# Routed attention and a quick-gelu feed-forward on one core: scores with the keys on the partitions, and two heads side by side

## The chip, the cores and the metric

The kernel runs on one core of a Trainium2 chip. The metric is the device time in microseconds of one launch.

## What is computed

The reference is an attention in which a query sees only the keys of its own cluster, and behind it a feed-forward block without routing:

```python
# q, k, v: (4, 8, 768, 64); centroids: (8, 16, 64); all normal numbers times 0.1
q_assign = argmax(normalised(q) @ normalised(centroids).T)     # also k_assign
mask = q_assign[:, :, :, None] == k_assign[:, :, None, :]
scores = np.where(mask, q @ k.T / 8, -1e9)
attn = exp(scores - max(scores)); attn /= sum(attn) + 1e-9
x = (attn @ v).transpose(0, 2, 1, 3).reshape(3072, 512)
h = x @ w_in                                                   # 512 x 2048
out = (h * sigmoid(1.702 * h)) @ w_out                         # 2048 x 512
```

Everything is float32, except that the two weight matrices come as float64 words.

## The kernel before, in words

There are 4 batches of 8 heads. Two heads are a pair; 16 pairs, 4 to a batch. A sequence is 6 tiles of 128 tokens, two halves of 384. A unit is one query tile of one head, so a pair has 12 units (UP) and the whole kernel 192 (NU).

Engines: TensorE (PE) multiplies and transposes, VectorE (DVE) and ScalarE (ACT) read its results out of PSUM, GpSimd (POOL) works on SBUF alone, SyncE (SP) issues the loads and stores. Each takes its instructions in the order in which the program below emits them (`manual_schedule`); only waits for data and for free buffers shift them.

Preparation of a pair (`PREP`, eleven steps, one per turn of the loop): `prep_qk` (L199) turns q and k so that the head dimension lies on the partitions, `prep_assign` (L218) multiplies each token tile with the 16 centroids of its head (24 matmuls of 16 columns) and finds the largest on DVE, `prep_hot` (L241) turns the one-hot codes and puts them as 16 extra rows under q and k. A matmul over 80 rows then gives the score, lowered by 2^100 where the clusters differ.

A unit: `scores` (L277) makes 128 queries x 768 keys in two matmuls of 384 columns. `softmax` takes the row maximum on DVE (L286), scales it (L288), and ACT writes the exponential and its row sum (L292). `normalise` divides: a reciprocal on DVE (L303), a scaling of all 768 columns on POOL (L304). `turn` (L314) transposes the six 128 x 128 blocks on PE, and ACT (L319) and DVE (L321) copy them out. `values` (L333) multiplies six value tiles, 64 columns wide, with the six blocks; ACT copies the result into x transposed (L336).

Feed-forward (FFN): when a batch is complete, 56 chunks are queued: 32 of `first` (L351: four matmuls of 384 columns, tanh on ACT L356, product on DVE L359) and 24 of `second` (L370: four matmuls of 512 columns; every fourth is followed by a copy L376 and a store). They use two PSUM banks of their own.

Weights come in 64 chunks of 128 x 256. `round_w` makes float32 of each in nine steps that go to and fro between the engines: DVE L130, L132, POOL L135, DVE L141, POOL L137, L139, DVE L143, L145, POOL L147. One or two chunks are done in each turn until all 64 are (in the 43rd turn), so that all of it lies in batch 0, where no FFN work exists yet.

The loop fixes the order of everything. In turn u it emits the scores of unit u, the scaling of u - 1, the transposes of u - 2, the softmax of u, then as many FFN chunks as are owed (4/3 a turn), the values of u - 3, one preparation step for the next pair, and the weights:

```python
    for u in range(NU + 3):
        ...
            scores(u)
        ...
            normalise(u - 1)
        ...
            turn(u - 2)
        ...
            softmax(u)
        owed = owed + rate if ffn else 0.0
        while owed >= 1.0 and ffn:
            ffn.popleft()()
            owed -= 1.0
        if u >= 3:
            values(u - 3)
        if p + 1 < NPAIR and r < len(PREP):
            PREP[r](p + 1)
```

So units 0 to 47 run without FFN work, the others with that of the batch before, and the FFN of the last batch is left for the end.

Of the kernel before, what the change touches and what calls it, by code (L numbers as in the profile page):

```python
# [8 lines left out]
FP32 = mybir.dt.float32  # L9
BF16 = mybir.dt.bfloat16  # L10
I32 = mybir.dt.int32
U32 = mybir.dt.uint32
# [2 lines left out]
AX = mybir.AxisListType  # L15


@with_exitstack
def kernel(
    ctx: ExitStack,  # L20
    tc: tile.TileContext,
    q: bass.AP,
# [4 lines left out]
    moe_w_out: bass.AP,  # L27
    out: bass.AP,
):
    """Routed attention, then x -> quick-gelu(x @ w_in) @ w_out, all in float32.  # L30

    The weights come as the 64-bit words of float64 numbers, which no engine
    computes with, and are rounded to float32 on the chip.

    Token s of a (batch, head) sits on partition s // NJ, at place s % NJ, so
    that each partition loads one contiguous run. Token tiles are the NJ places.
    """
    nc = tc.nc

    B, H, S, D = q.shape  # L40
    NC = centroids.shape[1]
    DM, DF = moe_w_in.shape
    P = 128
    NJ = S // P            # token tiles of a sequence
    HALF = S // 2          # score columns in one PSUM bank
    NH = NJ // 2           # token tiles of a half
    HP = H // 2            # head pairs
    NPAIR = B * HP
    NCH = DM // P
    NF = DF // P  # L50
    KA = D + NC            # contraction rows of the scores
    SLOT = 32              # columns of a one-hot code in its transpose
    SCALE = D ** -0.5
    # A key of another cluster gets -FAR added to its raw score, and the sum
    # rounds to -FAR exactly: its softmax weight is 0 next to any key of the
    # query's cluster, and where there is none all weights are equal.
    FAR = float(2 ** 100)
    assert D == 64 and NC == 16 and H * NC == P and NJ == 6 and DM == H * D

# [13 lines left out]
    ps_f = ctx.enter_context(tc.tile_pool(name="ps_f", bufs=2, space=PS))  # L73
    ctx.enter_context(tc.manual_schedule())

# [1 line left out]
    qk_in, v_in = {}, {}  # L77

    def pair_src(src, p):
# [4 lines left out]
    def load_qk(p):  # L84
        for w, src in enumerate((q, k)):
            t = inp.tile([P, 2, NJ, D], FP32, name=f"in{w}")
            nc.sync.dma_start(out=t.rearrange("p a j d -> p a (j d)"),
                              in_=pair_src(src, p))
            qk_in[p, w] = t

    def load_v(p):
        t = inp.tile([P, 2, NJ, D], FP32, name="inv", bufs=3)
        nc.sync.dma_start(out=t.rearrange("p a j d -> p a (j d)"),
                          in_=pair_src(v, p))
        v_in[p] = t
# [7 lines left out]

    w_in = const.tile([P, NCH, DF], FP32, name="w_in")
    w_out = const.tile([P, NF, DM], FP32, name="w_out")
    WN = 256               # weights per partition in a chunk
    w_chunks = [
        (w[:, c, n:n + WN],
         src.bitcast(I32)[c * P:(c + 1) * P, 2 * n:2 * (n + WN)])
# [10 lines left out]
            w_raw[i] = t  # L120

    def round_w(i):
        """float64 words to float32: +-2^k (a power in float32, 0 or inf past
        its range) times 1.m, of m the 20 high bits exactly, the rest rounded."""
        raw = w_raw.pop(i)
        hi, lo = raw[:, :, 1], raw.bitcast(U32)[:, :, 0]
        m, e, one_m = (hp_pool.tile([P, HALF], FP32, name="g")[:, 0:WN]
                       for _ in range(3))
        m, e = m.bitcast(I32), e.bitcast(I32)
        nc.vector.tensor_scalar(out=m, in0=hi, scalar1=0xFFFFF, scalar2=None,  # L130
                                op0=ALU.bitwise_and)
        nc.vector.tensor_scalar(out=e, in0=hi, scalar1=20, scalar2=0x7FF,  # L132
                                op0=ALU.logical_shift_right,
                                op1=ALU.bitwise_and)
        nc.gpsimd.tensor_scalar(out=one_m, in0=m, scalar1=2.0 ** -20,  # L135
                                scalar2=1.0, op0=ALU.mult, op1=ALU.add)
        nc.gpsimd.tensor_scalar(out=e, in0=e, scalar1=896 + 255.0,  # L137
                                scalar2=896.0, op0=ALU.min, op1=ALU.max)
        nc.gpsimd.tensor_scalar(out=e, in0=e, scalar1=-896.0, scalar2=1.0,  # L139
                                op0=ALU.add, op1=ALU.mult)  # L140
        nc.vector.scalar_tensor_tensor(out=one_m, in0=lo, scalar=2.0 ** -52,  # L141
                                       in1=one_m, op0=ALU.mult, op1=ALU.add)
        nc.vector.tensor_scalar(out=e, in0=e, scalar1=23, scalar2=None,  # L143
                                op0=ALU.logical_shift_left)
        nc.vector.scalar_tensor_tensor(out=e, in0=hi, scalar=-2 ** 31, in1=e,  # L145
                                       op0=ALU.bitwise_and, op1=ALU.bitwise_or)
        nc.gpsimd.tensor_tensor(out=w_chunks[i][0], in0=one_m,  # L147
                                in1=e.bitcast(FP32), op=ALU.mult)

    for i in range(3):  # L150
        load_w(i)

# [1 line left out]
    ident = const.tile([P, P], FP32, name="ident")  # L154
    masks.make_identity(nc, ident)
    ident_h = const.tile([P, P], BF16, name="ident_h")
    nc.vector.tensor_copy(out=ident_h, in_=ident)
    half = const.tile([P, 1], FP32, name="half")
    nc.vector.memset(half, 0.5)
    # NC - c for cluster c: the largest among equals is the first of them.  # L160
    rank = const.tile([P, NC], FP32, name="rank")
    nc.gpsimd.iota(rank, pattern=[[-1, NC]], base=NC, channel_multiplier=0,
                   allow_small_or_imprecise_dtypes=True)
    # One-hot codes before their transpose; the columns past NC stay 0.
    hot = [const.tile([P, NJ * 4, SLOT], BF16, name=f"hot{i}")
           for i in range(2)]
    for t in hot:
        nc.vector.memset(t, 0.0)

    # Normalised centroids, transposed: [D, H * NC].  # L170
    csq = const.tile([P, D], FP32, name="csq")
    css = const.tile([P, 1], FP32, name="css")
    nc.vector.tensor_tensor(out=csq, in0=cent, in1=cent, op=ALU.mult)
# [11 lines left out]
    nc.tensor.transpose(out=cps[0:D, 0:P], in_=csq, identity=ident)  # L185
    nc.vector.tensor_copy(out=cT, in_=cps[0:D, 0:P])

    # ---- operands of the scores: rows 0:D are q^T or k^T, rows D:KA the
    # cluster one-hot of a query, or FAR below 0 off the cluster of a key ----
    aug = {}  # L190

    def prep_qk(p, i):
# [13 lines left out]
            nc.vector.tensor_copy(out=dst, in_=ps[0:D, 0:HALF])  # L206

    def prep_assign(p):
        """The cluster of each token, as a one-hot code. The norm of q or k
        scales a token's NC products alike, so their order needs none."""  # L210
        hp = p % HP
        ps = ps_t.tile([P, 512], FP32, name="t")
        sc = ps[:, 0:NJ * 4 * NC].rearrange("p (n c) -> p n c", c=NC)
        for j in range(NJ):
            for w in range(2):
                for a in range(2):
                    c0 = (2 * hp + a) * NC
                    nc.tensor.matmul(  # L218
                        out=sc[:, 4 * j + 2 * w + a, :],
                        lhsT=aug[p, a][0:D, w, j * P:(j + 1) * P],  # L220
                        rhs=cT[:, c0:c0 + NC], start=True, stop=True)
        n = NJ * 4
        best = asg.tile([P, n], FP32, name="best")
        nc.vector.tensor_reduce(out=best, in_=sc, axis=AX.X, op=ALU.max)
        eq = asg.tile([P, n, NC], FP32, name="eq")
        nc.vector.tensor_tensor(
            out=eq, in0=sc, in1=best[:, :, None].broadcast_to((P, n, NC)),
            op=ALU.is_equal)
        nc.vector.tensor_tensor(
            out=eq, in0=eq, in1=rank[:, None, :].broadcast_to((P, n, NC)),  # L230
            op=ALU.mult)
        first = asg.tile([P, n], FP32, name="first")
        nc.vector.tensor_reduce(out=first, in_=eq, axis=AX.X, op=ALU.max)
        nc.vector.tensor_tensor(
            out=hot[p % 2][:, :, 0:NC], in0=eq,
            in1=first[:, :, None].broadcast_to((P, n, NC)), op=ALU.is_equal)
# [21 lines left out]
    PREP = [lambda p, i=i: prep_qk(p, i) for i in range(8)]  # L258
    PREP += [prep_assign, lambda p: None, prep_hot]

# [1 line left out]
    UH = NJ  # L262
    UP = 2 * NJ
    NU = NPAIR * UP
# [57 lines left out]
        AT_of[u] = AT  # L322

    def values(u):
        """A query tile's part of x^T: rows are model dims, columns tokens."""
        p, a, qt = split(u)
        AT = AT_of.pop(u)
        if a == 0 and qt == 0:
            xT_of[p] = xp.tile([P, S], FP32, name="xT", bufs=2 * NCH)
        O = ps_t.tile([P, 512], FP32, name="t")  # L330
        rows = slice(a * D, (a + 1) * D)
        for kt in range(NJ):
            nc.tensor.matmul(out=O[rows, 0:P], lhsT=v_in[p][:, a, kt, :],  # L333
                             rhs=AT[:, kt, :],
                             start=(kt == 0), stop=(kt == NJ - 1))
        nc.scalar.copy(xT_of[p][rows, qt * P:(qt + 1) * P], O[rows, 0:P])  # L336
        if u % (HP * UP) == HP * UP - 1:
            ffn.extend(ffn_chunks(p // HP))

# [1 line left out]
    ffn = deque()  # L341

    def ffn_chunks(b):
# [1 line left out]
        hs, ys = {}, {}  # L345

        def first(h, f):
            """2 * quick-gelu: x * sigmoid(1.702 x) = x / 2 * (1 + tanh(0.851 x))."""
            ps = ps_f.tile([P, 512], FP32, name="f")
            for c in range(NCH):  # L350
                nc.tensor.matmul(out=ps[:, 0:HALF],  # L351
# [34 lines left out]
                       for part in range(NF // 4)]  # L386
        return chunks

    # ---- program: the stages of a unit run in different turns of the loop,
    # and the next pair's operands and the last batch's products fill in ----  # L390
    for step in PREP:
        step(0)
    rate = (2 * NF + NJ * (NF // 4)) / (HP * UP - 6)
# [60 lines left out]
```

## Time and profile before

| | |
|---|---|
| time of three runs | 1738.17, 1742.84, 1749.67 us; median 1742.84 |
| span of the profiled execution | 1739.4 us, 3.4 us below that median |
| busy | PE 1627.0 us (94%), DVE 640.5, ACT 462.5, POOL 313.4 |
| instructions | 18961 |
| chain that ended last | PE 84%, DVE 8%, POOL 4%, ACT 2% |

The profile is of one execution. PE is its matmuls; "PEld" is the loading of weights into the array, which overlaps them. [...] A float32 matmul stands as two records, its two passes. Matmul ends are modelled and neighbours overlap in the records, so that the price of one is best read from start to start.

### The profile page before, as it was taken

The numbers are of one execution on the slowest core, as the hardware profiler recorded it, in microseconds if no ns is written. First come the engines' busy times: TensorE is split into PE (matmuls) and PEld (weight loads), VectorE is DVE, ScalarE is ACT, GpSimd is POOL, SyncE is SP. The second block draws the span as 40 slices with busy tenths as digits, with TensorE's granted clock in tenths as the row PEclk, the third lists the DMA queues.
The fourth block names the chain that finished last, engine by engine and source line by source line (L and its number), as shares of the span: only waits on it lengthen the run. The fifth ranks groups of instructions, "written<-read, shape, count | busy, mean of one in ns | idle before, by whom it ended". The sixth has DMA issues, their size and how long they took to land.

```text
span 1739.4 us, 18961 instructions
## 1 busy us (share of the span) xinstructions
PE 1627.0 (94%) x7265; PEld 1057.5 (61%) x7265; DVE 640.5 (37%) x1594; ACT 462.5 (27%) x1017; POOL 313.4 (18%) x456
## 2 busy tenths in 40 slices
PE   7787877889999999999999999999999999999999
PEld 5665655566666675566666566566666566556453
DVE  4666575744332333234332333224332333221020
ACT  1222231333231323223232232223232232221010
POOL 1556464621010101011110110101010111110000
PEclk9868586889899999989899998999999998999999
DMA  3122121200000000000000000000000000000000
GB/s 108 65 62 76 55 70 52 76 10 28 1 10 31 16 19 1 22 25 19 10 9 14 30 21 1 16 31 19 10 10 6 13 1 1 7 13 0 12 6 18
DMA packets 25962, 43.20 MB, mean 25 GB/s; under 512 B 2320, under 2 KB 14608, under 8 KB 25872
## 3 DMA queue, kind: packets, MB, share of 16 engines
q1 hardware_dynamic: 25728, 41.95, 7.6%
q8 instruction: 58, 0.95, 0.2%
q14 instruction: 32, 0.26, 0.0%
q10 hardware_dynamic: 144, 0.03, 0.0%
HBM read 35.68 MB, written 6.29 MB: 24 GB/s over the span
## 4 chain that ended last, share of the span: by engine, by line
PE 84%; DVE 8%; POOL 4%; ACT 2%; issue 1%; DMA 0%; ACTq 0%; DVEq 0%
PE f L351 20%; PE f L370 19%; PE t L333 15%; PE s L277 14%; PE t L314 7%; PE t L218 6%; PE t L199 3%; DVE aug L252 2%; POOL g L137 2%; ACT aug L256 1%; DVE AT L321 1%; DVE mx L286 1%; DVE g L145 1%; POOL g L139 1%; POOL g L135 1%
## 5 line engine op out<-in xcount | busy, mean ns | idle before, releaser
L304 POOL TENSOR_SCALAR A<-A,rec 128x768 f32<-128x768 f32 x192 | 173.8, 905 | 1107.9 <-DVE rec L303 1072.9
L351 PE MATMUL f<-xT,w_in 128*128 128x384 f32 x1024 | 357.5, 502 | 0.0
L333 PEld LDWEIGHTS t<-AT,inv 128*64 128x64 f32 x2304 | 268.4, 146 | 133.7 <-issue 66.6
L333 PE MATMUL t<-AT,inv 128*64 128x128 f32 x2304 | 317.4, 292 | 32.8 <-ACT AT L319 27.0
L370 PE MATMUL f<-w_out,g 128*128 128x512 f32 x768 | 344.5, 599 | 0.0
L277 PE MATMUL s<-aug 80*128 80x384 f32 x768 | 331.7, 560 | 2.7 <-DVE aug L252 2.7
L351 PEld LDWEIGHTS f<-xT,w_in 128*128 128x128 f32 x1024 | 196.0, 198 | 123.0 <-issue 14.0
L292 ACT ACTIVATE A<-s,bias 128x768 f32<-128x768 f32 x192 | 172.8, 900 | 261.8 <-DVE bias L288 261.8
L370 PEld LDWEIGHTS f<-w_out,g 128*128 128x128 f32 x768 | 144.0, 193 | 159.0 <-issue 156.9
L314 PEld LDWEIGHTS t<-ident,A 128*128 128x128 f32 x1152 | 153.1, 154 | 118.9 <-issue 83.1
L319 ACT COPY AT<-t 128x384 f32<-128x384 f32 x192 | 91.8, 478 | 479.1 <-PE t L314 479.1
L314 PE MATMUL t<-ident,A 128*128 128x128 f32 x1152 | 182.1, 296 | 39.5 <-DVE aug L252 32.7
L321 DVE COPY AT<-t 128x384 f32<-128x384 f32 x192 | 106.3, 554 | 299.1 <-PE t L314 298.6
L277 PEld LDWEIGHTS s<-aug 80*128 80x128 f32 x768 | 149.6, 217 | 76.2 <-issue 31.1
L359 DVE SCALAR_TENSOR_TENSOR g<-th,f 128x384 f32<-128x384 f32 x128 | 70.9, 554 | 318.4 <-ACT th L356 318.4
L286 DVE TENSOR_REDUCE mx<-s 128x1 f32<-128x768 f32 x192 | 182.0, 948 | 2.6 <-PE s L277 2.6
L218 PE MATMUL t<-cT,aug 64*128 64x16 f32 x768 | 111.6, 293 | 4.7 <-DVE AT L321 4.7
L336 ACT COPY xT<-t 64x128 f32<-64x128 f32 x192 | 49.5, 258 | 247.9 <-PE t L333 247.1
L218 PEld LDWEIGHTS t<-cT,aug 64*128 64x128 f32 x768 | 109.9, 229 | 7.9 <-DVE AT L321 5.2
L356 ACT ACTIVATE th<-f 128x384 f32<-128x384 f32 x128 | 62.8, 490 | 145.9 <-PE f L351 145.9
L199 PE MATMUL t<-ident,in 128*64 128x128 f32 x384 | 72.5, 305 | 19.9 <-DVE AT L321 18.6
L206 DVE COPY aug<-t 64x384 f32<-64x384 f32 x64 | 35.1, 548 | 105.5 <-PE t L199 105.5
(46 smaller groups left out, 587.1 us busy)
## 6 DMA issues: line engine op xcount, KB each, us to landing
raw<-in_moe_w_in_dram SPq DMA_DIRECT2D x32, 256.0 KB, 2.8
raw<-in_moe_w_out_dram SPq DMA_DIRECT2D x32, 256.0 KB, 2.7
in<-in_q_dram SPq DMA_DIRECT2D x16, 384.0 KB, 3.5
in<-in_k_dram SPq DMA_DIRECT2D x16, 384.0 KB, 4.0
inv<-in_v_dram SPq DMA_DIRECT2D x16, 384.0 KB, 3.2
out_dram<-y SPq DMA_DIRECT2D x24, 256.0 KB, 2.0
cent<-in_centroids_dram ACTq DMA_DIRECT2D x1, 32.0 KB, 1.9
```

The source lines that it names most:

```text
L199: nc.tensor.transpose(out=ps[0:D, n * P:(n + 1) * P], in_=qk_in[p, w][:, a, h * NH + n, :], identity=ident)
L218: nc.tensor.matmul(out=sc[:, 4 * j + 2 * w + a, :], lhsT=aug[p, a][0:D, w, j * P:(j + 1) * P], rhs=cT[:, c0:c0 + NC], start=True, stop=True)
L277: nc.tensor.matmul(out=ps[:, h, 0:HALF], lhsT=t[:, 0, qt * P:(qt + 1) * P], rhs=t[:, 1, h * HALF:(h + 1) * HALF], start=True, stop=True)
L286: nc.vector.tensor_reduce(out=mx, in_=s, axis=AX.XY, op=ALU.max)
L292: nc.scalar.activation(out=A.rearrange("p (h n) -> p h n", h=2), in_=s, func=AF.Exp, bias=bias, scale=SCALE, accum_out=den)
L304: nc.gpsimd.tensor_scalar(out=A, in0=A, scalar1=rec[:, 0:1], scalar2=1.0, op0=ALU.mult, op1=ALU.mult)
L314: nc.tensor.transpose(out=ps[:, n * P:(n + 1) * P], in_=A[:, kt * P:(kt + 1) * P], identity=ident)
L319: nc.scalar.copy(dst, ps[:, 0:HALF])
L321: nc.vector.tensor_copy(out=dst, in_=ps[:, 0:HALF])
L333: nc.tensor.matmul(out=O[rows, 0:P], lhsT=v_in[p][:, a, kt, :], rhs=AT[:, kt, :], start=(kt == 0), stop=(kt == NJ - 1))
L351: nc.tensor.matmul(out=ps[:, 0:HALF], lhsT=w_in[:, c, f * P:(f + 1) * P], rhs=xT[c][:, h * HALF:(h + 1) * HALF], start=(c == 0), stop=(c = ...
L370: nc.tensor.matmul(out=ps[:, 0:DM], lhsT=hs[h, f][:, n * P:(n + 1) * P], rhs=w_out[:, f, :], start=(f == 0), stop=(f == NF - 1))
```

## The change

The kernel becomes `fast`, and the kernel before stays as `general` behind a branch that is taken where a check of the softmax sums fails (`bad`).

In `fast` a unit is one key tile and one query half of both heads: a pair again has 12 units. The queries' T tile holds both heads, head 0 on partitions 0 to 63 and head 1 on 64 to 127. `scores` multiplies 128 keys with 384 queries, once for each head, over 64 rows of the array each, into two PSUM banks. The keys are on the partitions, so the exponentials (no maximum is subtracted) can go into the values matmul as they are: no transposes and copies. The mask is a product on DVE: a query's cluster code, spread over all partitions, is compared with the key's own, and the result multiplies the exponential (one operation per head). The sums over keys are added up tile by tile on POOL, and at the end of a query half a matmul with ones adds the 128 partitions. `values` writes head 0 to partitions 0 to 63 and head 1 to 64 to 127 of one bank, over six units. The division is done once per query half, on the 64 values of a head.

```diff
+    bad = fast(tc, *args)
+    with tc.If(bad > 0):
+        general(tc, *args)
...
-    ps_s = ctx.enter_context(tc.tile_pool(name="ps_s", bufs=2, space=PS))
-    ps_t = ctx.enter_context(tc.tile_pool(name="ps_t", bufs=2, space=PS))
-    ps_f = ctx.enter_context(tc.tile_pool(name="ps_f", bufs=2, space=PS))
+    ps_s = ctx.enter_context(tc.tile_pool(name="ps_s", bufs=2, space=PS))
+    ps_o = ctx.enter_context(tc.tile_pool(name="ps_o", bufs=1, space=PS))
+    ps_m = ctx.enter_context(tc.tile_pool(name="ps_m", bufs=3, space=PS))
...
+    def prep_near(p):
...
+        for w in range(2):
+            for h in range(2):
+                r = 32 * (2 * w + h)
+                nc.tensor.matmul(
+                    out=ps[r:r + 32, 0:HALF],
+                    lhsT=cT[:, p % HP].rearrange("p a c -> p (a c)"),
+                    rhs=T[p, w][:, h * HALF:(h + 1) * HALF],
+                    start=True, stop=True)
...
+    def prep_spread(p):
...
+        line = dram.tile([n, P], BF16, name="line")
+        nc.sync.dma_start(out=line, in_=row)
+        qb = trp.tile([P, 2, S], BF16, name="qb")
+        nc.sync.dma_start(
...
+    PREP = [lambda p, i=i: prep_turn(p, i) for i in range(4)]
+    PREP += [prep_near, prep_assign, lambda p: None, prep_spread]
...
+    def scores(u):
+        p, h, kt = split(u)
+        ps = ps_s.tile([P, 2, 512], FP32, name="s")
+        for a in range(2):
+            rows = slice(a * D, (a + 1) * D)
+            nc.tensor.matmul(out=ps[:, a, 0:HALF],
+                             lhsT=T[p, 1][rows, kt * P:(kt + 1) * P],
+                             rhs=T[p, 0][rows, h * HALF:(h + 1) * HALF],
+                             start=True, stop=True)
...
+        nc.scalar.activation(out=A, in_=s_of.pop(u), func=AF.Exp, scale=SCALE)
+        for a in range(2):
+            nc.vector.scalar_tensor_tensor(
+                out=A[:, a, :],
+                in0=qcode[p][:, a, h * HALF:(h + 1) * HALF],
+                scalar=code[p][:, kt % NH, 1, kt // NH, a:a + 1],
+                in1=A[:, a, :], op0=ALU.is_equal, op1=ALU.mult)
...
+        nc.gpsimd.tensor_tensor(out=sum_of[g], in0=first, in1=A_of[u],
+                                op=ALU.add)
...
+        for a in range(2):
+            nc.tensor.matmul(out=o_of[g][a * D:(a + 1) * D, 0:HALF],
+                             lhsT=v_in[p][:, a, kt, :], rhs=A[:, a, :],
+                             start=(kt == 0), stop=(kt == NJ - 1))
...
+    def normalise(g):
...
+        for a in range(2):
+            nc.tensor.matmul(out=ps[a * D:(a + 1) * D, 0:HALF], lhsT=ones,
+                             rhs=sm[:, a, :], start=True, stop=True)
+        rec = op.tile([P, HALF], FP32, name="rec")
+        nc.vector.reciprocal(out=rec, in_=ps[:, 0:HALF])
...
+    LAG = 2
+    DEN = 4
...
+    is_bad = nc.values_load(bad[0:1, 0:1], min_val=0, max_val=1)
+    while ffn:
+        ffn.popleft()()
+    return is_bad
```

The FFN is the same code but for its banks: it shares three (`m`) with the preparation and the denominators. q and k are now loaded head by head, in pieces of 256 bytes, so that the two heads of a token lie side by side.

In the program's order three places matter. First PE in the mixed stage, one turn and the next scores. Before (s scores, t the banks of `turn`, `values` and the preparation, f the FFN):

```order
L277 MATMUL s<-aug 128x384 x2
L314 MATMUL t<-ident,A 128x128 x6
L351 MATMUL f<-xT,w_in 128x384 x4
L333 MATMUL t<-AT,inv 64x128 x6
L199 MATMUL t<-ident,in_3679 64x128 x3
L277 MATMUL s<-aug 128x384 x2
```

Now (L319 scores, L397 FFN, L357 values into bank o, L231 the turning of q and k, L372 the denominators):

```order
L319 MATMUL s<-T_4600,T_4662 128x384 x2
L397 MATMUL m<-xT,w_in 128x384 x4
L357 MATMUL o<-A,inv 64x384 x2
L372 MATMUL m<-sum,ones 64x384 x2
L231 MATMUL m<-ident,in_4582 128x128 x3
L319 MATMUL s<-T_4600,T_4662 128x384 x2
```

The six transposes are gone, the values are two wide matmuls instead of six narrow ones, and the denominators come in every sixth turn.

Second, POOL in the first stage, one turn with one weight chunk and the start of the next. Before (L304 the scaling):

```order
L304 TENSOR_SCALAR A<-A,rec 128x768
L135 TENSOR_SCALAR g<-g 128x256
L137 TENSOR_SCALAR g<-g 128x256
L139 TENSOR_SCALAR g<-g 128x256
L147 TENSOR_TENSOR w_in<-g 128x256
```

Now (L347 the sum over key tiles, L158 to L170 the same four steps of a chunk):

```order
L347 TENSOR_TENSOR sum<-sum,A 128x768
L158 TENSOR_SCALAR g<-g 128x256
L160 TENSOR_SCALAR g<-g 128x256
L162 TENSOR_SCALAR g<-g 128x256
L170 TENSOR_TENSOR w_in<-g 128x256
```

In the place of the one-input scaling stands a two-input sum. Third, PE at the end of the attention. Now, with the check's transpose (L476) and the load of its result into a register (L482):

```order
L319 MATMUL s<-T_4891,T_4951 128x384 x2
L357 MATMUL o<-A,inv 64x384 x6
L372 MATMUL m<-sum,ones 64x384 x2
L476 MATMUL m<-ident,ok_5440 1x128
L482 TENSOR_LOAD bad
L397 MATMUL m<-xT,w_in 128x384 x64
```

Before, the last values were followed by the 64 matmuls of the FFN at once; now the check stands between them.

## Rows read from the trace of the kernel before

**Rows 1.** The page: busy time by engine; granted clock in forty slices, tenths.
```profile
PE 1627.0 (94%) x7265; PEld 1057.5 (61%) x7265; DVE 640.5 (37%) x1594; ACT 462.5 (27%) x1017; POOL 313.4 (18%) x456
...
PEclk9868586889899999989899998999999998999999
```

**Rows 2.** Stretches: length, busy by engine, clock, DMA share, GB/s.
```profile
32.40:385.20 352.80, 283.99 (x1332) 209.15 (x1331) 219.88 (x603) 92.40 (x212) 181.60 (x304) 0.77 0.19 59
385.20:1183.80 798.60, 777.92 (x3634) 504.05 (x3633) 266.47 (x633) 232.17 (x508) 86.94 (x96) 0.95 0.05 16
1183.80:1570.40 386.60, 378.40 (x1770) 242.72 (x1768) 126.14 (x304) 113.62 (x251) 43.47 (x48) 0.96 0.03 9
1570.40:1739.40 169.00, 165.20 (x449) 85.01 (x448) 17.73 (x32) 19.55 (x39) 0.00 (x0) 1.00 0.03 10
```

**Rows 3.** Stretches, the exponentials (L292) alone: ACT busy and records.
```profile
32.40:385.20 352.80, 47.57 (x96) 0.77 0.19 59
385.20:1183.80 798.60, 95.15 (x192) 0.95 0.05 16
```

**Rows 4.** Chain that ended last, from the last scores: start, length, what.
```profile
1559.97 0.97 PE s L277 x3
...
1570.45 41.48 PE f L351 x128
1611.92 41.20 PE f L370 x96
```

**Rows 5.** Timeline of PE, one turn of the mixed stage: start, length, what.
```profile
799.55 1.46 PE L277 MATMUL s<-aug 80*128 80x384 f32 x4
800.84 0.82 PE L314 MATMUL t<-ident,A 128*128 128x128 f32 x6
801.50 2.75 PE L351 MATMUL f<-xT,w_in 128*128 128x384 f32 x8
804.17 1.52 PE L333 MATMUL t<-AT,inv 128*64 128x128 f32 x12
805.63 0.52 PE L199 MATMUL t<-ident,in 128*64 128x128 f32 x3
805.98 1.46 PE L277 MATMUL s<-aug 80*128 80x384 f32 x4
```

**Rows 6.** Timeline of PE around a pair's centroid matmuls.
```profile
833.94 5.83 PE L218 MATMUL t<-cT,aug 64*128 64x16 f32 x48
839.70 2.93 PE L277 MATMUL s<-aug 80*128 80x384 f32 x4
```

**Rows 7.** Groups of instructions: operation and count, busy us, mean ns, idle before.
```profile
L304 POOL TENSOR_SCALAR A<-A,rec 128x768 f32<-128x768 f32 x192 | 173.8, 905 | 1107.9 <-DVE rec L303 1072.9 <-PE t L333 24.9 <-PE t L314 10.0
...
L359 DVE SCALAR_TENSOR_TENSOR g<-th,f 128x384 f32<-128x384 f32 x128 | 70.9, 554 | 318.4 <-ACT th L356 318.4
...
L135 POOL TENSOR_SCALAR g<-g 128x256 f32<-128x256 int32 x64 | 25.9, 404 | 75.8 <-DVE g L130 74.0
...
L147 POOL TENSOR_TENSOR w_in<-g 128x256 f32<-128x256 f32 x32 | 23.2, 725 | 27.9 <-DVE eps L300 18.3 <-DVE g L145 9.6
```

**Rows 8.** DMA issues: KB each, us from issue to landing.
```profile
inv<-in_v_dram SPq DMA_DIRECT2D x16, 384.0 KB, 3.2
out_dram<-y SPq DMA_DIRECT2D x24, 256.0 KB, 2.0
```

**Rows 9.** Timeline of DVE, then POOL, in the first stage.
```profile
139.13 0.28 DVE L130 TENSOR_SCALAR g<-raw 128x256 int32<-128x256 int32 x1
139.33 0.28 DVE L132 TENSOR_SCALAR g<-raw 128x256 int32<-128x256 int32 x1
...
141.81 0.29 DVE L130 TENSOR_SCALAR g<-raw 128x256 int32<-128x256 int32 x1
142.01 0.84 DVE L132 TENSOR_SCALAR g<-raw 128x256 int32<-128x256 int32 x1
...
141.97 0.72 POOL L147 TENSOR_TENSOR w_in<-g 128x256 f32<-128x256 f32 x1 [0.87 <-DVE g L145]
```

343 lines of the change are left out of this document (342 added, 1 removed).

## The prediction

> **What bounds the kernel now.** Read the page first: TensorE (PE) is busy 1627 of 1739.4 us, and from the eleventh of forty slices on its granted clock shows eight or nine tenths and more [rows 1]. One average hides four stages, so the table of stretches comes next [rows 2]: 32.4 us of prologue; 352.8 us of attention for batch 0 beside the rounding of the weights; 798.6 and 386.6 us of attention with the two products of the batch before (FFN) mixed in; 169.0 us of FFN of the last batch alone. PE is busy 80% of the second, at a mean clock of 0.77, and 97 to 98% of the third and fourth, at 0.95 and 0.96. The exponentials, two records each, count the units [rows 3]: 48 units in 352.8 us, 7.35 us a unit; 96 in 798.6 us, 8.32 us a unit. So an engine beside PE is worth nothing in the mixed stage, and PE work is worth little in the first.
>
> The FFN alone gives the price of PE work [rows 4]: 41.48 us for 128 passes of 384 columns, 0.324 us each; 41.20 for 96 passes of 512, 0.429 each. A float32 matmul is two passes (128 records are 64 matmuls in the order). A batch is 2 x (41.48 + 41.20) = 165.4 us, 3.45 us per mixed unit (165.4 / 48). The other 8.32 - 3.45 = 4.87 us are attention and preparation. One turn shows them, start to start [rows 5]: scores 1.29 (4 passes, 0.32 each), six transposes 0.66, FFN chunk 2.67, values 1.46 (12 passes of 128 columns), three preparing transposes 0.35.
>
> The matmuls against the centroids (L218) are 16 columns wide, yet 48 passes take 5.76 us, and the scores behind them 2.93 us in place of 1.46 [rows 6]: half clock after them. This is where the 0.95 loses.
>
> **The mixed stage, 144 units.** Goes: the transposes of A, 0.66 a unit; L218, 5.76 / 12 = 0.48, and with it most of that clock loss. Scores keep two matmuls of 384 columns, K 64 instead of 80. Values become two of 384 columns: four passes, 1.30 serially, against 1.46. Preparation per pair, in passes of 384 at 0.324: nearest centroids 8 (2.6 us), denominators 8 (2.6), and 16 transposes at 0.35 / 3 = 0.12 (1.9), 7.1 / 12 = 0.59 a unit.
>
> Changing the shape of the array has a price in the turn: the FFN chunk takes 2.67 where 8 x 0.324 = 2.59, values 1.46 where 12 x 0.11 (0.66 / 6) = 1.32, so 0.08 + 0.14 around the narrow values. Scores now are in a half-height shape too. That is not shown; bounds 0 to 0.3, I charge again 0.22. Values followed by preparation costs another 0.06 on the average.
>
> Without any overlap of halves a unit is 1.30 + 1.30 + 0.59 + 0.5 + 0.2 for waits and clock = 3.89, and 7.34 with the FFN.
>
> What the two halves gain is not in the trace: no two neighbours there use different halves at work. Bounds: nothing, or half of the time. The order on PE is head 0 (pass 1, pass 2), head 1 (pass 1, pass 2). Passes start in order, and head 0's second needs its first out of the way, so head 1's first can only run beside head 0's second: three pass times in place of four. I take this. Scores and values save 0.324 each; the four-part centroid matmuls go from 8 to 5 pass times, the denominators from 8 to 6, together 5 x 0.324 / 12 = 0.14. A unit: 7.34 - 0.79 = 6.55.
>
> [...]
>
> Stretches of 96 and 48 units at 8.32 and 8.05: saved 96 x 1.77 + 48 x 1.52 (6.53 in the last, which prepares one pair less) = **243 us**; serially 96 x 0.98 + 48 x 0.75 = **130**.
>
> Cover: per unit VectorE (DVE) has two products of 384 columns, taken as 0.554 each like L359 [rows 7], and some 1 us more; ScalarE (ACT) one exponential, at most 95.15 / 96 = 0.99 [rows 3], and copies; GpSimd (POOL) 5/6 of a sum. All are far below 6.55 and two turns ahead of the values. The code line's way through DRAM is 2.0 + 3.2 us by the nearest landings [rows 8] and starts four units early.
>
> **The first stage, 48 units: nothing, -50 to +40.** DVE and POOL hand each weight chunk to and fro: from one L130 to the next 2.68 us [rows 9], 1.5 chunks a unit, 4.0 us. Its softmax work (reduction, bias, reciprocal, copy, about 2 us) becomes the two products, 1.11. But POOL's one-input scaling, 0.905 for 768 columns, becomes a sum with two inputs. POOL takes 404 ns for 256 columns with one input and 725 with two (L135, L147) [rows 7]; one-input work has 404 - (905 - 404) / 2 = 154 ns fixed, so 768 columns with two inputs cost 154 + 3 x 571 = 1.87 us. Bounds: 725 + 501 = 1.23 and 3 x 725 = 2.18. The sum stands in front of the first rounding step on POOL and behind the products, so DVE waits for nearly all of it: 1.87 x 5/6 = 1.56. Also L132 takes 0.84 instead of 0.28 while L147 runs [rows 9]: a POOL operation with two inputs holds such a DVE operation, 0.56 a hit, 0.4 a unit. With preparation and the denominators' three DVE operations, about 0.6 (the wide reciprocal taken as 0.55; doubled, 0.1 more), a unit is 1.11 + 4.0 + 1.56 + 0.4 + 0.6 = 7.7 for 43 units, less some waits for L218; then five free ones of about 5. 43 x 7.7 + 25 = 356, against 352.8. PE's gain is hidden here.
>
> **Ends: +4 us, 0 to +10.** Prologue 0 (-5 to +8): L218 falls from 10 us to 5, the code line's two transfers add 5, and loads in 256-byte pieces queue ahead of them. Before the last FFN stands a new chain from the last scores: exponential 1, products 1.1, sum 1.9, denominators 1.3, three DVE steps 1.7, the check's five short steps about 1, a register load that no row shows (0.5 to 3); on PE all 224 FFN matmuls of the last batch are queued behind that load. That is 9 to 11 us, and 1559.97 to 1570.45 was 10.5 [rows 4]. The branch at the end: 1 to 3.
>
> **Sum.** 1739.4 - 243 + 0 + 4 = 1500. The median of the runs is 3.4 above this span, so 1504.
>
> **Rivals.**
> 1. The halves do not overlap: 1739.4 - 130 + 4 + 3.4 = 1617. For it: no row shows a pass that runs beside another. Against: nothing. If only one of scores and values overlaps: about 1560.
> 2. Both halves start together: per unit another 0.65, and preparation 5 passes / 12 = 0.14 less, 5.76 a unit: 0.79 x 144 = 114 more, 1390. Against: the order of the passes.
> 3. Slower: the clock. Half of the array works in every scores and values pass, and the half-height L218 is followed by half clock [rows 6]; in stage one, PE at 80% busy got 0.77 [rows 2]. Serially the turn is 7.14 at full clock; at 0.77 it is 9.27, and 144 x (9.27 - 8.23) = 150 us are lost, 8.23 being the old mean of 1185.2 / 144: 1897. It decides below 7.14 / 8.23 = 0.87 (0.77 if passes overlap). Against: values were half-width in each old turn, and the clock was 0.95; half of each new turn is FFN on the full array.
> 4. The check fails and the general path runs behind the fast one: over 3200. Against: 768 keys over 16 clusters from normal numbers leave no cluster of a query empty. I give it nothing.
>
> **How the numbers follow.** Three pass times 0.55 (own range 1445 to 1565: 50 for the first stage, 0.2 a unit for shapes), serial 0.26, one kind only 0.06, together 0.06, clock 0.07. The range 1430 to 1650 leaves out rival 2, rival 3 and the upper quarter of rival 1, together two in ten. The runs spread by 0.7%, so 1% is about what a measurement can tell from no change. Rival 3 gives slower 0.05 and, with a clock near its point, same 0.02; the rest is faster, 0.93.
>
> **What would show it.** In the mixed stage a unit of 6.55 us; scores and values with 0.97 between their first start and the next matmul's (1.30: rival 1; 0.65: rival 2); a clock above 0.95, else rival 3. POOL's sum at 1.87, and DVE waiting for it in stage one, whose 48 units stay within 300 to 395 us. I am wrong if stage one gives most of the gain, or if the mixed stage waits for DVE, ACT or the three shared banks.

## The result and the profile after

The changed kernel takes 1362.39 us (median; 1362.01 to 1363.19) against 1743.55 for the kernel before: the ratio of the two sets of runs is 0.7803, 95% interval 0.7771 to 0.7836 (the medians alone divide to 0.7814). The forecast was 1504 us, in a range from 1430 to 1650. The direction was right, the size was not: it lies beyond the low end of the range, and beyond even rival 2 (1390). In the experiments, the times of `e5_pe_sums` to `e8_check_last` are medians of four executions and the others single ones; one execution of `e6_spread` took 3745.13 us (without it the median would be 1332.29) and the kernel before, beside `e9_order_0011` to `e11_values_apart`, once took 3133.11, neither with a known cause.

The stretches of the changed kernel that answer to [rows 2], cut at the exponentials of units 0, 48 and 144 and 0.4 us behind the last FFN's start (length, then PE, PEld, DVE, ACT and POOL busy, clock, DMA share, GB/s):

```profile
0.00:15.30 15.30, 7.29 (x30) 3.80 (x30) 5.80 (x20) 2.72 (x4) 1.35 (x8) 0.90 0.84 208
15.30:362.10 346.80, 181.99 (x502) 54.93 (x500) 227.49 (x469) 47.98 (x67) 223.91 (x294) 0.70 0.23 68
362.10:907.80 545.70, 543.48 (x1922) 231.10 (x1924) 245.68 (x392) 135.19 (x212) 147.15 (x81) 1.00 0.11 28
907.80:1185.00 277.20, 270.30 (x946) 114.31 (x947) 121.74 (x193) 66.64 (x104) 74.13 (x41) 0.99 0.07 19
1185.00:1360.30 175.30, 167.44 (x448) 85.97 (x447) 17.73 (x32) 19.26 (x38) 0.00 (x0) 0.98 0.03 10
```

| stage | before | after | difference | forecast |
|---|---|---|---|---|
| until unit 0 | 32.4 | 15.3 | -17.1 | 0 |
| first stage, 48 units | 352.8 | 346.8 | -6.0 | 0 |
| mixed stage, 144 units | 1185.2 | 822.9 | -362.3 | -243 |
| last FFN and end | 169.0 | 175.3 | +6.3 | +4 |
| span | 1739.4 | 1360.3 | -379.1 | -239 |

In the mixed stage PE is still busy nearly all the time, now at a granted clock of 1.00 and 0.99 (1.00 without a break from 367 to 1179 us; the lower value that the trace shows is 0.50, as from 1181 to 1189 us). One turn of it on PE's timeline, with one FFN chunk and three preparing transposes, answers to [rows 5]:

```profile
700.22 0.92 PE L319 MATMUL s<-T,T 64*128 64x384 f32 x4
701.07 2.85 PE L397 MATMUL m<-xT,w_in 128*128 128x384 f32 x8
703.84 0.87 PE L357 MATMUL o<-A,inv 128*64 128x384 f32 x4
704.64 0.55 PE L231 MATMUL m<-ident,in 128*128 128x128 f32 x3
705.12 0.92 PE L319 MATMUL s<-T,T 64*128 64x384 f32 x4
```

From start to start the scores' four passes take 0.85 us (1.29 before), the values' four 0.80 (1.46 for twelve), and the turn 4.90 instead of 6.43. Four passes one behind the other would need 1.29: both heads are done in two pass times (0.65) and a change of shape (0.20; the FFN chunk, on the whole array, takes 0.18 more than its eight pass times). In the records behind this view the scores' passes start in twos, 6 to 7 ns apart, the second two 0.43 us after the first.

The groups of instructions on the other engines that the forecast priced (mean ns after the busy us) answer to [rows 7]:

```profile
L331 DVE SCALAR_TENSOR_TENSOR A<-qb,code,A 128x384 f32<-128x384 bf16 x384 | 259.5, 718 | 247.3 <-ACT A L329 242.4 <-DMA qb<-line 4.9
L347 POOL TENSOR_TENSOR sum<-sum,A 128x768 f32<-128x768 f32 x128 | 233.7, 1826 | 437.5 <-DVE A L331 437.5
...
L375 DVE RECIPROCAL rec<-m 128x384 f32<-128x384 f32 x32 | 81.7, 2553 | 34.6 <-PE m L372 34.6
...
L170 POOL TENSOR_TENSOR w_out<-g 128x256 f32<-128x256 f32 x32 | 29.9, 933 | 27.9 <-DVE g L168 27.9
```

### The profile page after: what moved, and what is told of

Read it like the earlier page. It is cut to its first block, busy times and chain, and to the rows that moved or that the text cites. A ratio compares the mean times of both kernels' runs of the same rounds, so it can differ in the third digit from the quotient of the medians.

```text
span 1360.3 us, 10636 instructions
## 1 busy us (share of the span) xinstructions
PE 1170.5 (86%) x3842; PEld 490.1 (36%) x3842; DVE 618.4 (45%) x1104; ACT 271.8 (20%) x425; POOL 446.5 (33%) x424
## 5 line engine op out<-in xcount | busy, mean ns | idle before, releaser
L347 POOL TENSOR_TENSOR sum<-sum,A 128x768 f32<-128x768 f32 x128 | 233.7, 1826 | 437.5 <-DVE A L331 437.5
L331 DVE SCALAR_TENSOR_TENSOR A<-qb,code,A 128x384 f32<-128x384 bf16 x384 | 259.5, 718 | 247.3 <-ACT A L329 242.4
L357 PE MATMUL o<-A,inv 128*64 128x384 f32 x768 | 228.8, 569 | 158.7 <-DVE A L331 139.1
L397 PE MATMUL m<-xT,w_in 128*128 128x384 f32 x1024 | 353.9, 497 | 1.5 <-DVE bad L480 1.1
L416 PE MATMUL m<-w_out,g 128*128 128x512 f32 x768 | 345.3, 600 | 0.0
L329 ACT ACTIVATE A<-s 128x768 f32<-128x768 f32 x192 | 155.6, 810 | 529.7 <-PE s L319 497.6
L397 PEld LDWEIGHTS m<-xT,w_in 128*128 128x128 f32 x1024 | 189.8, 191 | 160.5 <-issue 26.9
L416 PEld LDWEIGHTS m<-w_out,g 128*128 128x128 f32 x768 | 141.6, 190 | 185.4 <-issue 182.6
L319 PE MATMUL s<-T,T 64*128 64x384 f32 x768 | 194.0, 585 | 0.0
L357 PEld LDWEIGHTS o<-A,inv 128*64 128x64 f32 x768 | 52.8, 147 | 319.5 <-DVE A L331 190.6
L347 POOL TENSOR_TENSOR sum<-A 128x768 f32<-128x768 f32 x32 | 59.5, 1860 | 196.4 <-DVE A L331 194.2
L375 DVE RECIPROCAL rec<-m 128x384 f32<-128x384 f32 x32 | 81.7, 2553 | 34.6 <-PE m L372 34.6
L319 PEld LDWEIGHTS s<-T,T 64*128 64x128 f32 x768 | 63.8, 204 | 87.0 <-issue 72.3
L164 DVE SCALAR_TENSOR_TENSOR g<-raw,g 128x256 f32<-128x256 uint32 x64 | 27.2, 425 | 62.8 <-POOL g L158 62.8
L231 PE MATMUL m<-ident,in 128*128 128x128 f32 x192 | 39.4, 323 | 0.3 <-DMA in<-in_k_dram 0.2
L170 POOL TENSOR_TENSOR w_out<-g 128x256 f32<-128x256 f32 x32 | 29.9, 933 | 27.9 <-DVE g L168 27.9
L170 POOL TENSOR_TENSOR w_in<-g 128x256 f32<-128x256 f32 x32 | 29.5, 923 | 27.9 <-DVE g L168 27.9
```

Source lines behind the costliest of these rows:

```text
L170: nc.gpsimd.tensor_tensor(out=w_chunks[i][0], in0=one_m, in1=e.bitcast(FP32), op=ALU.mult)
L319: nc.tensor.matmul(out=ps[:, a, 0:HALF], lhsT=T[p, 1][rows, kt * P:(kt + 1) * P], rhs=T[p, 0][rows, h * HALF:(h + 1) * HALF], start=True, ...
L329: nc.scalar.activation(out=A, in_=s_of.pop(u), func=AF.Exp, scale=SCALE)
L331: nc.vector.scalar_tensor_tensor(out=A[:, a, :], in0=qcode[p][:, a, h * HALF:(h + 1) * HALF], scalar=code[p][:, kt % NH, 1, kt // NH, a:a ...
L347: nc.gpsimd.tensor_tensor(out=sum_of[g], in0=first, in1=A_of[u], op=ALU.add)
L357: nc.tensor.matmul(out=o_of[g][a * D:(a + 1) * D, 0:HALF], lhsT=v_in[p][:, a, kt, :], rhs=A[:, a, :], start=(kt == 0), stop=(kt == NJ - 1))
```

## The experiments

The theory: two matmuls in different halves of the array run side by side, so a pair of heads costs two pass times, and since PE alone bounds the mixed stage, 144 units gain all of it. The rival: the 6 ns are only times of issue, and the gain comes from the transposes and narrow matmuls that went. A second theory concerns the first stage: what holds it at 347 us when half of its PE time is idle.

**Both heads apart** (`e1_apart`).

```diff
-            scores(u)
+            scores(u, (0,))
...
+            values(u - LAG, (0,))
         while owed >= 1.0 and ffn:
             ffn.popleft()()
             owed -= 1.0
+            scores(u, (1,))
...
+            values(u - LAG, (1,))
```

> The changed kernel with its two heads never next to each other on PE: scores of head 0 and values of head 0 stand ahead of the turn's FFN chunks, scores and values of head 1 behind them. The work is the same. Overlap theory: a pair of heads took two pass times and now takes four, 8 passes a unit instead of 4 pass times, 4 x 0.322 = 1.29 us, and two more changes of the array's shape, about 0.2; 144 mixed units lose 215 us: about 1575 us, and the two passes of one head stand 0.32 apart with nothing beside them. Rival (the 6 ns starts in the trace are only issue times, the gain comes from what was removed): only the two shape changes cost, 144 x 0.2 = 29, at most 60: 1390 to 1420.

Measured: 1615.54 us, 253 more. Without the overlap the kernel is next to rival 1's 1617. A lone score matmul, half of the work, takes as long as the pair did (0.84 us to the next kind, 0.85 for the pair). PE's timeline of this kernel, around one FFN chunk:

```profile
804.82 0.91 PE L321 MATMUL s<-T,T 64*128 64x384 f32 x2
805.66 0.86 PE L361 MATMUL o<-A,inv 128*64 128x384 f32 x2
806.45 0.91 PE L321 MATMUL s<-T,T 64*128 64x384 f32 x2
807.29 0.86 PE L361 MATMUL o<-A,inv 128*64 128x384 f32 x2
808.08 2.85 PE L401 MATMUL m<-xT,w_in 128*128 128x384 f32 x8
```

Two passes stand where four stood, in 0.84 and 0.79 us. Splitting adds 0.84 + 0.79 = 1.63 a unit, 235 us over 144; the mixed stage measures 240 us more, and the first stage, 12 us longer, gives most of the rest. The theory holds. Of the 1.63, four pass times are 1.29 and the other 0.34 changes of shape, where 0.2 were expected; that and the first stage are the excess over 215.

**One kind apart.** `e2_scores_apart` splits the scores alone, `e11_values_apart` the values alone, by the same edit.

> Only the scores' heads stand apart (head 0 ahead of the FFN chunks, head 1 behind), the values stay side by side. Overlap theory, if row halves and column halves gain alike: 144 x (0.64 + 0.1) = 107 us, about 1470. If only the column halves (values) overlap: 1362 + 15 to 30. If the rows alone do: about 1575, as with both apart.

> Only the values' heads stand apart (head 0 ahead of the FFN chunks, head 1 behind), the scores stay side by side. If column halves gain as row halves did (scores apart: 110 us more): about 1470. The rest of the 253 us that both apart cost would put it at 1505 at most; if columns do not overlap, below 1400.

Measured: 1471.77 and 1461.00, 109 and 99 more. Row halves and column halves gain nearly alike.

**The transposes put back** (`e3_transposes`).

```diff
+        if UP * HP <= u < NU:
+            for i in range(2):
+                x = bank()
+                for n in range(NH):
+                    nc.tensor.transpose(out=x[:, n * P:(n + 1) * P],
+                                        in_=T[p, i][:, n * P:(n + 1) * P],
+                                        identity=ident)
```

> The changed kernel with six 128 x 128 transposes added to each of the 144 mixed units (of the pair's own turned q and k, into two banks that nobody reads), as many as the old kernel had. If PE alone bounds the mixed stage: 6 x 0.109 = 0.65 and some 0.1 for a change of shape, 144 x 0.66 to 0.76 = 95 to 110 us, about 1460 to 1470. Rival (the mixed stage has PE time to spare): less than 40 us, below 1400.

Measured: 1472.18, 110 more, 0.76 a unit. The mixed stage has no PE time to spare. So of the 362 us gained there, the overlap accounts for about 186 (four pass times a unit, by `e1_apart`) and the six transposes for 110; the rest, the narrow centroid matmuls and the clock above all, was not tested apart.

**The order of the heads.** `e10_order_0101` and `e9_order_0011` issue each score matmul twice; the edit of the second is shown, the first has (0, 1, 0, 1).

```diff
-        for a in range(2):
+        for a in (0, 0, 1, 1):
```

> Each score matmul of the changed kernel is issued twice (the second writes the same scores again), in the order head 0, head 1, head 0, head 1. Two neighbours in different halves go together: 4 pass times instead of 2 in a unit, 144 x 2 x 0.32 = 93 us more and a little in the first stage: about 1455 to 1470.

> The same four score matmuls in the order head 0, head 0, head 1, head 1. If matmuls start strictly in program order and only neighbours pair up: head 0 alone, then the middle two together, then head 1 alone, 6 pass times, 144 x 4 x 0.32 = 185 us more than the changed kernel, about 1545 to 1555. If passes rather than matmuls are what goes in order (each half has a queue of its own and works through it independently): 4 pass times as in the alternating order, about 1460. If one half may run ahead by one pass only: 5, about 1505.

Measured: 1451.46 for the alternating order and 1453.64 for the other. PE's timeline, first of `e10_order_0101`, then of `e9_order_0011`; eight passes each:

```profile
700.80 1.56 PE L319 MATMUL s<-T,T 64*128 64x384 f32 x8
702.30 2.85 PE L397 MATMUL m<-xT,w_in 128*128 128x384 f32 x8
```

```profile
701.20 1.57 PE L319 MATMUL s<-T,T 64*128 64x384 f32 x8
702.69 2.85 PE L397 MATMUL m<-xT,w_in 128*128 128x384 f32 x8
```

1.50 and 1.49 us, four pass times and a change of shape both. The second pair adds 0.65 us to the 0.85 of one pair: two pass times, not three. With head 0's two matmuls in front six pass times would be 1.94 us; 1.49 leaves no time in which head 1's wait for head 0's. Over these four score matmuls program order did not hold one half back for the other; the values' column halves were not tried in this order, and what orders the passes was not measured.

**Four fifths of POOL's sums left out** (`e4_no_sums`).

```diff
-        if u % NJ == 0:
+        if u % NJ != 1:
             return
```

> Four of the five sums over key tiles in each query half are left out on POOL (the denominators are then those of two tiles, and the check passes or fails as it did). If these sums bind the first stage together with the rounding: 1.83 us on POOL in 4 of 6 units, of which DVE waits about 1.6, and no holding of the DVE products, 43 x (1.1 to 1.6) = 45 to 70 us less, about 1295 to 1315 us; the mixed stage stays. Rival (the hand-over of the rounding between DVE and POOL binds alone, and the sums lie in its gaps): above 1345 us.

Measured: 1323.03, 39 less, between theory and rival. The first stage is 311.8 us in place of 346.8, so each of its 32 sums left out was worth 1.1 us, not 1.6. The timeline of the changed kernel, DVE and POOL, shows how a sum delays the rounding, and that the products and POOL hold one another:

```profile
100.23 0.28 DVE L155 TENSOR_SCALAR g<-raw 128x256 int32<-128x256 int32 x1
100.25 1.93 POOL L347 TENSOR_TENSOR sum<-sum,A 128x768 f32<-128x768 f32 x1 [0.56 <-DVE A L331]
...
102.26 0.40 POOL L158 TENSOR_SCALAR g<-g 128x256 f32<-128x256 int32 x1
...
102.70 0.43 DVE L164 SCALAR_TENSOR_TENSOR g<-raw,g 128x256 f32<-128x256 uint32 x1 [2.19 <-POOL g L158]
...
105.99 0.43 DVE L164 SCALAR_TENSOR_TENSOR g<-raw,g 128x256 f32<-128x256 uint32 x1 [0.38 <-POOL g L158]
...
107.86 1.61 DVE L331 SCALAR_TENSOR_TENSOR A<-qb,code,A 128x384 f32<-128x384 bf16 x2
...
108.03 1.03 POOL L170 TENSOR_TENSOR w_in<-g 128x256 f32<-128x256 f32 x1 [0.87 <-DVE g L168]
```

The sum stands in front of L158, and L164 on DVE idles 2.19 us for it, where it idles 0.38 without a sum in front. Two products beside L170 take 1.61 us, where a pair alone takes 1.15, and L170 1.03 where it takes 0.72 alone.

**Sums on PE in batch 0** (`e5_pe_sums`), **one weight chunk a turn** (`e6_spread`), **both** (`e7_both`, with u + 1 for u). Beside what is shown, the denominators of batch 0 then come two turns earlier, and the spread rounding gets its own pool for its three work tiles; what that pool alone is worth was not measured.

```diff
+        if g < 2 * HP:
+            for a in range(2):
+                nc.tensor.matmul(out=den_of[g][a * D:(a + 1) * D, 0:HALF],
+                                 lhsT=ones, rhs=A[:, a, :],
+                                 start=(kt == 0), stop=(kt == NJ - 1))
...
-        while w_next < min(len(w_chunks), (3 * u + 1) // 2):
+        while w_next < min(len(w_chunks), u):
```

> In batch 0 alone (units 0 to 47) POOL's sums are gone: PE multiplies each masked tile with the ones at once and adds up over the six key tiles in a bank, one pair of matmuls a unit more. If POOL's sums delay the rounding in the first stage (leaving out four fifths of them took 35 us off it): 40 sums at 1.1 us, 44 us less, and PE's 0.65 to 1.3 us more a unit lies in its idle time: about 1318 us, first stage near 300. Rival (the array's time at the lower clock binds as soon as the sums go, PE has been waiting and waking in turns): no gain, 1345 to 1375.

> The rounding goes one weight chunk a turn instead of one and a half (64 turns instead of 43; its three work tiles get a pool of their own, with two buffers for one of them and one for the others), so 16 of 64 chunks fall into the mixed stage. If the hand-over between DVE and POOL binds the first stage: 16 x 2.7 to 3.3 us = 43 to 53 less, about 1315 us, the mixed stage staying PE-bound. Rival (the moved chunks delay the mixed stage's turns, whose DVE then has products, rounding and gelu in 5.7 us): gain below 15 us.

> Both edits: PE sums in batch 0 and one chunk a turn. A first-stage unit is then 1.22 for the products, 2.7 to 3.2 for one chunk, 1.0 for the rest of DVE, about 5.2, 48 x 5.2 = 250 us against 347: about 1265 to 1280. Rival (PE at the lower clock needs 2 x (0.85 + 0.8 + 0.75) + preparation, about 5.5 to 6 a unit, and binds): 1290 to 1310.

Measured: 1317.07, 1332.75 and 1275.13 us (0.7535, 0.7626 and 0.7298 of the kernel before). The first is as forecast. The second falls between theory and rival: the first stage drops to 283.4 us, 63 less, but the next 96 units take 578.7 instead of 545.7, so 33 us come back where moved rounding meets the mixed stage: all of them in the first 24 of these units, in which the rounding ends. Together they do what was expected.

**The check moved into the last FFN** (`e8_check_last`), on top of both edits.

```diff
+    while len(ffn) > 36:
+        ffn.popleft()()
     ok = const.tile([P, 2 * NPAIR], FP32, name="ok")
...
+    while len(ffn) > 20:
+        ffn.popleft()()
     is_bad = nc.values_load(bad[0:1, 0:1], min_val=0, max_val=1)
```

> As both edits, and the check's five steps and the register load stand among the last FFN's chunks instead of ahead of them. If the load ahead of the FFN costs what the trace shows (PE waits from the last denominators to the FFN 6.4 us, of which 2.6 are the check): 2 to 3 us less than the kernel with both edits. Rival (PE's wait for the register inside the FFN costs as much): no difference.

Measured: 1267.00 us, 0.7251 of the kernel before (0.7194 to 0.7307), 8.1 less than without the move: more than expected. The end of the attention in the changed kernel:

```profile
1177.81 0.87 PE L372 MATMUL m<-sum,ones 128*64 128x384 f32 x4 [1.11 <-POOL sum L347]
...
1183.12 0.37 PE L476 MATMUL m<-ident,ok 128*1 128x128 f32 x1 [4.45 <-DVE ok L474]
...
1184.57 7.75 PE L397 MATMUL m<-xT,w_in 128*128 128x384 f32 x15 [1.08 <-DVE bad L480]
```

And with the check moved:

```profile
1091.33 0.87 PE L383 MATMUL m<-sum,ones 128*64 128x384 f32 x4 [1.11 <-POOL sum L348]
1092.12 8.33 PE L408 MATMUL m<-xT,w_in 128*128 128x384 f32 x25
```

The FFN's first chunks read only the first query half and need nothing of the last denominators. The load had held them for the whole chain: from the denominators to the FFN 6.8 us instead of 0.8. After that idle time the first 15 passes took 7.75 us, at a granted clock of 0.50 until 1190.0 us, where with the check moved 25 take 8.33. The stages of this fastest version:

```profile
15.30:255.90 240.60, 178.22 (x658) 60.30 (x656) 179.50 (x382) 47.98 (x67) 112.81 (x183) 0.87 0.27 79
255.90:821.40 565.50, 550.32 (x1926) 233.03 (x1928) 286.34 (x479) 135.37 (x212) 189.34 (x152) 0.99 0.13 36
```

The first stage is 106 us shorter than in the changed kernel; the mixed stage gives 20 us back.

## Why the prediction was wrong, and where it was right

- **The failing step** is in the mixed stage: "Passes start in order, and head 0's second needs its first out of the way, so head 1's first can only run beside head 0's second: three pass times in place of four. I take this." It is two. From the first start to the next kind 0.97 us was forecast and 0.85 (scores) and 0.80 (values) were measured, two pass times of 0.65 and a change of shape. `e1_apart`, `e2_scores_apart` and `e11_values_apart` show the halves side by side (253, 109 and 99 us more where they stand apart), the second pair of `e10_order_0101` costs 0.65, and in `e9_order_0011` the four score matmuls took 1.49 us after 1.50 in the alternating order, so the program order on which the step rested did not bind one half to the other there. By the forecast's own numbers this is worth 0.79 x 144 = 114 of the 140 us by which the sum was off; the other 26 are the prologue (17), the first stage (6) and 5 more in the mixed stage, less 2 at the end. Rival 2 had the mechanism and for the mixed stage the size: 357 us by its numbers, 362 measured. I gave it 0.06 because I took the order of starts, 0.32 us apart in the turn of [rows 5], to hold between the halves as well, an estimate that no row showed.
- **Prologue, 0 forecast, -17.1 measured.** L218's 10 us became not 5 but 1.43 (L248 below). Four column quarters work side by side: in the mixed stage their eight passes take 0.78 us to the next matmul, two pass times (0.65) and a change of shape, where eight pass times would be 2.58. And the scores of unit 0 do not wait for the code line; only the products do, 4.9 us, and that wait falls in the first stage. Three more steps were not in the forecast: the centroid matmuls start 3.1 us earlier (8.28, not 11.35), nothing stands between the codes and the scores (L241 to L277, 3.5 us before), and the first scores reach their exponential in 1.7 us, not 4.2. PE before:

```profile
11.35 10.42 PE L218 MATMUL t<-cT,aug 64*128 64x16 f32 x48
24.78 0.82 PE L241 MATMUL t<-ident_h,hot 128*128 128x128 bf16 x6 [3.02 <-DVE hot L234]
28.26 2.93 PE L277 MATMUL s<-aug 80*128 80x384 f32 x4 [2.67 <-DVE aug L252]
```

And the changed kernel's first microseconds:

```profile
8.28 1.43 PE L248 MATMUL m<-T,cT 128*32 128x384 f32 x8
...
13.66 1.65 PE L319 MATMUL s<-T,T 64*128 64x384 f32 x4
...
18.87 1.15 DVE L331 SCALAR_TENSOR_TENSOR A<-qb,code,A 128x384 f32<-128x384 bf16 x2 [4.88 <-DMA qb<-line]
```

- **Right: PE bounds the mixed stage**, and nothing else takes over (543.48 of 545.70 us busy, and the transposes put back cost 110 us, 0.76 a unit, their whole time). The clock rival fell: 1.00 where it was 0.95, with half-array matmuls in every turn. In the kernel before, each pair's centroid matmuls in the mixed stage were followed, 2 to 6 us after their start, by 7 to 10 us at a granted clock of 0.50; that they caused it was not tested apart.
- **Right: the first stage gains next to nothing** (-6.0), with POOL's sum as the reason (1.83 us, forecast 1.87). Two terms were off inside it, and that they point opposite ways is luck: a sum delays the stage by 1.1 us net, 0.9 a unit rather than 1.56, and the wide reciprocal is 2.55 us, not 0.55, 0.33 more a unit.
- **Right: shapes.** Forecast 0.5 a unit. In the turn shown the scores take 0.20 us more than their pass times, the FFN chunk 0.18 and the values 0.15, together 0.53. In the records both ends of a kind show it: its second pass starts 0.37 to 0.43 us behind its first, and the next kind 0.41 to 0.42 behind its last, where passes of a kind follow at 0.32.
- **Right: the ends in sum** (forecast +4; measured +6.3, without the prologue). The chain ahead of the last FFN was foreseen as a wait as long as the old one, and from the last scores to the FFN it is 11.8 us after 11.0 before. The last FFN starts at a granted clock of 0.50, and from the last store's issue to the end pass 7.1 us instead of 3.1. What the forecast did not ask is whether the FFN has to wait for the check at all; moved away, the check gave back 8.1.

## What to carry to other kernels

Two small float32 matmuls in different halves of the array cost as much here as one when they stand next to each other (0.85 us for the scores of two heads, 0.84 for one), and with four of them the order made no difference (1.50 and 1.49 us in the two tried); with an FFN chunk between the two they cost twice as much (0.84 each). Put the partners together and price the pair at two passes (0.65 us here), with the 0.15 to 0.2 us measured for the change of shape around them. A stage that PE does not bound needs its own look: here the remaining gain (95 us) was in a two-input sum on POOL that could move to an idle PE, in work that could be spread into the next stage, and in a check that stood in front of work which did not need it. Where a step of a forecast rests on an order that no row shows, it deserves a wide chance, not the point.

## What was not expected of the hardware

- In the records neighbours in different halves (L319, L357) or quarters (L248) start 4 to 8 ns apart, and four score matmuls took 1.50 us with the halves in turn and 1.49 with one half's two in front.
- In the records of the changed kernel a DVE product (L331) and a two-input POOL operation (L170 or L347) hold one another. A product takes 0.61 us alone. One that starts while the POOL operation runs ends 0.41 to 0.42 us after it: 1.08 us in all beside L170 (0.67 until L170's end), up to 2.17 beside L347 (1.75 until its end). One that has started ahead of L170 keeps its 0.61, and L170 goes from 0.72 to 1.03. The cause was not tested.
- A reciprocal of 384 columns takes 2553 ns on DVE, where the product of 384 columns L359 took 554 [rows 7].
